# Gated attention, GLU and routed experts in one kernel: three kinds of work moved from POOL to VectorE, and the routing pieces placed anew in the order of the groups

## The chip, the cores and the metric

The kernel runs on one core of a Trainium2 chip. Its time is the device time of one execution in microseconds (us); the time before is the median of three executions. Engines are named as in the profile: PE is TensorE (its weight loads are PEld), DVE is VectorE, ACT is ScalarE, POOL is GpSimd, SP is SyncE.

## The reference

Three layers follow one another on 3072 tokens (4 batches of 768) of width 384 (8 heads of 48), all in float32.

```python
for t in range(S):                                        # gated linear attention
    state = alpha[:, :, t, :, None] * state + np.einsum('bhd,bhe->bhde', k[:, :, t], v[:, :, t])
    y[:, :, t] = np.einsum('bhd,bhde->bhe', q[:, :, t], state)
...
x = ((x @ w_a) * (x @ w_b)) @ w_out                       # GLU, 384 -> 1536 -> 384
...
logits = x @ w_gate + modality_bias[modality_id]          # 8 experts, the best one takes the token
out[mask] = gate_w[mask, None] * (np.maximum(x[mask] @ w1[e], 0.0) @ w2[e])   # 384 -> 1024 -> 384
```

## The kernel before

Float32 products are made of three TensorE passes: each operand is split into a high part (a copy in fp32r on ACT, names ending in h) and a remainder (a subtraction, names ending in l), and high times high, high times low and low times high are summed.

**Groups.** The tokens are cut into eight groups (w = 0 to 7) of 384, each of three chunks of 128. A group goes through attention chunk by chunk and then through the GLU in 12 f-steps. An f-step has 18 matmuls `ab` (L723: x times 128 columns of w_a and of w_b), a copy `asb` of the first half (ACT, L728), the product `g` (DVE, L734), its high part `gh` (ACT, L736) and remainder `gl` (DVE, L741), and nine matmuls `px` of w_out (L693), which come one f-step later. Group 7 has no attention left beside it; after it come the experts.

**Order.** PE, DVE, ACT and SP execute in the order in which the code issues, and that order is written by hand in strings: SEQ for groups 0 to 2, STEADY once for each of groups 2 to 6. A line of STEADY is an f-step of group w; four lines hold a chunk of group w+1's attention, and the pieces of group w-1's routing are strewn in. The letters: m is `ab`, `asb`; p is `px`; g is `g`, `gh`; l is `gl`. The numbers 1, 2, 3 prepare a chunk on DVE: transposes of alpha, k and q (L397), the running products R (L419) and `at` (L430), `kt` (L428) and `qt` = q times `at` (L432). S is the scores `s` = `kt` by `qt` on PE (L444). M masks them to `sm`. V is the part on the state: in before the pads (`vpad`, ACT, L471), the decay `state` times R (L477) and `y` (PE, L492 to L513). H is `xh`, the high part of `y` (ACT, L525) and the transposed keys on PE (L535); X is its remainder `xl` (DVE, L529); T is `ktok` (ACT, L537); U is `u` (PE, L543) and its addition to the state (DVE, L559); D closes the chunk.

**Routing, R.** Each R is one piece of `route` (L764). For groups 1 to 5 (and 6, in a form of its own below) a logit is a product with a row of the gate matrix, summed along the row on DVE (`junk`, L771; 24 for a group, two to a piece). Then come the softmax and the one-hot choice `oh` (DVE, L789 to L810, one piece), the counts `rank` on PE (L815 to L819, one piece), and the positions `rk`, `posi`, `base` on DVE (L823 to L829) with three indirect DMAs by POOL (L832) that write the tokens' places into a table in HBM. Groups 0 and 7 make the logits on PE: three transposes `xT`, a copy on ACT, three small matmuls `L` for each 128 tokens (L779 to L786).

**Group 7 and the experts.** The table of groups 0 to 6 is read back (`rte`, SP, L1019) when group 6 has been routed. The first expert weights `w1re`, `w2re` are issued on SP behind that read; ACT makes their high parts (`w0he` to `w3he`, L1067), between the `asb` and `gh` of group 7; the remainders (L1068) are made on DVE, every fourth one on POOL. Three early slots of experts and nine late ones follow.

Of the kernel before, what the change touches and what calls it, by code (L numbers as in the profile page):

```python
# [20 lines left out]
P = 128  # L21
# [45 lines left out]
MIX = 5, 2, 3  # L67
# [6 lines left out]
def gla_moe_kernel(ctx, tc, q, k, v, alpha, w_a, w_b, w_out, modality_id, w_gate, modality_bias, w1, w2, out):  # L74
# [162 lines left out]
    def load_ids():  # L237
# [5 lines left out]
        idf = ap.tile([NT, P], F32, tag="sm", bufs=3, name="idf")  # L243
# [11 lines left out]
        t0 = ap.tile([P, NT, E], F32, tag="sm", bufs=3, name="bias0")  # L255
# [67 lines left out]
    class Attention:  # L323
# [79 lines left out]
        def prepare(self, c):  # L403
# [28 lines left out]
            (nc.vector if self.w < LATE else nc.gpsimd).tensor_tensor(qt, q0, at, op=ALU.mult)  # L432
# [40 lines left out]
        def decay(self, c):  # L473

            if self.gc(c):
                R = self.ready[c][0]
                (nc.gpsimd if self.w else nc.vector).tensor_tensor(  # L477
                    state, state, R.broadcast_to([P, NPAIR, 2 * D]), op=ALU.mult
                )

        def values(self, c):
# [7 lines left out]
            if later:  # L489
                for kk in range(2):  # L490
                    for i in range(2):
# [3 lines left out]
                        if not (kk or i or self.w < LATE):  # L495
# [165 lines left out]
    def tokens(*groups):  # L661
# [15 lines left out]
        names = dict(S=["scores"], M=["mask"], V=["pads", "decay", "values"], H=["high"], X=["low"], T=["keys"], U=["carry"], D=["add"])  # L677
        return {**{nm.upper(): turns(nm) for nm in "akq"}, **dict.fromkeys("123", p), **{t: each(*does) for t, does in names.items()}}

    def lazily(make):  # L680
        yield from make()
# [82 lines left out]
    def route(w, pool, puts, gate=None):  # L764
# [3 lines left out]
        for t in range(CPW):  # L768
# [7 lines left out]
            else:  # L776
# [3 lines left out]
                xt = pool.tile([P, 512], F32, tag="sm", bufs=3, name=f"xT{w}_{t}")[:, :DM]  # L780
# [227 lines left out]
    class Slot:  # L1008
# [44 lines left out]
        def split(self):  # L1053
# [3 lines left out]
            for j in range(2 * NF2):  # L1057
# [10 lines left out]
                (nc.gpsimd if j % 4 == 3 else nc.vector).tensor_tensor(l, src, h, op=ALU.subtract)  # L1068
# [171 lines left out]
    def clear_table():  # L1240
        fill = ap.tile([P, TAB // P * 2], F32, tag="sm", bufs=3, name="fill")
# [3 lines left out]
    def turn_gate():  # L1245
# [4 lines left out]
        t = ap.tile([P, 512], F32, tag="sm", bufs=3, name="gateT")[:E, :DM]  # L1250
# [3 lines left out]
    def pipeline(y_d=None):  # L1254
# [3 lines left out]
        with tc.tile_pool(name="att", bufs=1) as ap:  # L1258
# [19 lines left out]
            if y_d is None:  # L1278
                with tc.manual_schedule(engines={EN.DVE, EN.PE, EN.SP, EN.Activation}):
# [7 lines left out]
                    def second():  # L1287
# [5 lines left out]
                        clear_table()  # L1293
# [28 lines left out]
                    extra = {"r": rest, "i": load_ids(), "W": gate_turn(), "Z": chain(then_load(then), then_load(nxt)), "R": lazily(lambda: route(0, ap, puts))}  # L1322
                    todo = halves + [(w, f) for w in range(2, NW - 1) for f in range(NF)]
# [30 lines left out]
                    for w in range(2, NW - 1):  # L1354
# [200 lines left out]
```

## Time and profile before

| what | value |
|---|---|
| median of three executions | 867.98 us (867.7 to 869.49) |
| the profiled execution | 876.44 us |
| its span in the trace | 874.6 us, so 1.8 us lie outside the span |
| PE, DVE, ACT, POOL busy | 819.8, 674.0, 292.7, 206.0 us |
| chain of work that ended last | PE 61%, DVE 21%, issue 6%, ACT 3%, POOL 3%, DMA 2% |

The busy times are sums over the whole span; whether an engine waits in a stretch, and for whom, is read from the views of the waits and from the timeline. Durations are those of the one profiled execution, which took 8.5 us longer than the median.

### The profile page before, as it was taken

Reading aid. Unit: us, or ns where it says so; the run is one execution under the profiler, and the core shown is the slowest. Engines: PE = TensorE matmul, PEld = TensorE weight load, DVE = VectorE, ACT = ScalarE, POOL = GpSimd, SP = SyncE. Lnnn points to the kernel's source line nnn. Section 1 sums busy time; section 2 is a strip of 40 time slices with the busy share of each in tenths; the row PEclk is TensorE's granted clock in tenths of the full one; section 3 lists DMA queues with packets and bytes.
Section 4 is the critical chain, followed back from the end, with each engine's and each line's share of the span. In section 5 each row is a group of like instructions: output and inputs, shape, how many; then the busy total and the mean of one; then the engine's idle time right before and its main releaser. Section 6 shows DMA issues by size and latency. Waiting matters only on the chain.

```text
span 874.6 us, 16828 instructions
## 1 busy us (share of the span) xinstructions
PE 819.8 (94%) x6193; PEld 771.2 (88%) x6193; DVE 674.0 (77%) x1495; ACT 292.7 (33%) x684; POOL 206.0 (24%) x283
## 2 busy tenths in 40 slices
PE   7778999999999998999999999899799999999995
PEld 6667998988998998998899899899699998998994
DVE  7878898659887987998998888774569876675641
ACT  2233442331222222221222222121555565564640
POOL 5221100102111012111111111102426554555421
PEclk9899999999999999999999999999899999999998
DMA  9988842716412410422422220030943988695900
GB/s 170 195 191 201 209 123 73 195 52 81 110 28 63 107 50 2 136 56 54 118 64 64 62 59 1 2 100 2 385 130 137 326 313 275 184 362 162 314 33 23
DMA packets 127089, 113.93 MB, mean 130 GB/s; under 512 B 55919, under 2 KB 105875, under 8 KB 126996
## 3 DMA queue, kind: packets, MB, share of 16 engines
q1 hardware_dynamic: 116260, 100.57, 42.2%
q0 software_dynamic: 4480, 10.99, 3.6%
q10 hardware_dynamic: 6256, 1.19, 1.1%
q8 instruction: 51, 0.84, 0.5%
q14 instruction: 42, 0.34, 0.1%
HBM read 101.87 MB, written 11.00 MB: 129 GB/s over the span
## 4 chain that ended last, share of the span: by engine, by line
PE 61%; DVE 21%; issue 6%; ACT 3%; POOL 3%; DMA 2%; another core or an unknown queue 2%; SPq 1%; DVEq 0%; POOLq 0%; ACTq 0%
PE ab L723 19%; PE px L693 9%; PE hl L1155 9%; PE pol L1103 8%; DVE R L419 3%; DVE at L430 2%; DVE g L734 2%; PE he L1155 2%; PE poe L1103 2%; PE s L444 2%; PE u L543 2%; DVE junk L771 2%; DVE kt L397 2%; DVE qt L397 1%
## 5 line engine op out<-in xcount | busy, mean ns | idle before, releaser
L723 PE MATMUL ab<-xh,pa 128*128 128x384 f32 x576 | 166.0, 342 | 7.9 <-ACT asb L728 5.5
L723 PE MATMUL ab<-xh,pb 128*128 128x384 f32 x576 | 163.4, 337 | 3.5 <-DVE pb L225 2.8
L693 PE MATMUL px<-po,gh 128*128 128x384 f32 x576 | 148.3, 342 | 0.4 <-DVE po L225 0.4
L723 PEld LDWEIGHTS ab<-xh,pa 128*128 128x128 f32 x576 | 106.4, 189 | 9.6 <-ACT asb L728 5.8
L723 PEld LDWEIGHTS ab<-xh,pb 128*128 128x128 f32 x576 | 106.1, 189 | 5.4 <-DVE pb L225 3.7
L736 ACT ACTIVATE gh<-g 128x384 fp32r<-128x384 f32 x96 | 50.3, 524 | 172.7 <-DVE g L734 171.4
L693 PEld LDWEIGHTS px<-po,gh 128*128 128x128 f32 x576 | 101.8, 188 | 3.8 <-issue 1.0
L723 PE MATMUL ab<-xl,pa 128*128 128x384 f32 x288 | 97.2, 337 | 0.3
L723 PE MATMUL ab<-xl,pb 128*128 128x384 f32 x288 | 96.8, 336 | 0.0
L728 ACT ACTIVATE asb<-ab 128x384 f32<-128x384 f32 x96 | 46.9, 489 | 145.5 <-PE ab L723 143.5
L693 PE MATMUL px<-po,gl 128*128 128x384 f32 x288 | 94.4, 337 | 0.3 <-DVE gl L741 0.3
L734 DVE TENSOR_TENSOR g<-ab,asb 128x384 f32<-128x384 f32 x96 | 53.2, 554 | 50.6 <-issue 26.7
L1160 DVE SCALAR_TENSOR_TENSOR hll<-hl,hhl 128x256 fp32r<-128x256 f32 x72 | 30.3, 421 | 54.1 <-ACT hhl L1158 50.4
L771 DVE SCALAR_TENSOR_TENSOR junk<-xr,gate 128x384 bf16<-128x384 f32 x96 | 65.2, 679 | 2.4
L477 POOL TENSOR_TENSOR state<-state,R 128x384 f32<-128x384 f32 x18 | 16.1, 895 | 203.1 <-DVE R L419 193.9
L741 DVE TENSOR_TENSOR gl<-g,gh 128x384 fp32r<-128x384 f32 x96 | 54.0, 563 | 9.7 <-ACT gh L736 9.7
L723 PEld LDWEIGHTS ab<-xl,pa 128*128 128x128 f32 x288 | 54.6, 190 | 0.8 <-DVE xl L529 0.8
L693 PEld LDWEIGHTS px<-po,gl 128*128 128x128 f32 x288 | 53.8, 188 | 1.0 <-DVE gl L741 1.0
L723 PEld LDWEIGHTS ab<-xl,pb 128*128 128x128 f32 x288 | 54.5, 189 | 0.0
L1158 ACT ACTIVATE hhl<-hl 128x256 fp32r<-128x256 f32 x72 | 27.7, 384 | 63.4 <-PE hl L1155 55.0
L832 POOL DMA_INDIRECT tab_d<-rec,posi x24 | 24.2, 1009 | 89.7 <-DVE base L829 50.1
L432 POOL TENSOR_TENSOR qt<-qt,at 128x512 f32<-128x512 f32 x15 | 20.3, 1355 | 89.3 <-DVE qt L397 89.3
(340 smaller groups left out, 1871.4 us busy)
## 6 DMA issues: line engine op xcount, KB each, us to landing
w1rl<-in_moe_w SPq DMA_DIRECT2D x18, 768.0 KB
w2rl<-in_moe_w SPq DMA_DIRECT2D x18, 768.0 KB
raw_a<-in_alpha SPq DMA_DIRECT2D x72, 96.0 KB
raw_k<-in_k SPq DMA_DIRECT2D x72, 96.0 KB
raw_q<-in_q SPq DMA_DIRECT2D x72, 96.0 KB
wo<-in_moe_w_out SPq DMA_DIRECT2D x6, 768.0 KB
w1re<-in_moe_w SPq DMA_DIRECT2D x6, 768.0 KB
w2re<-in_moe_w SPq DMA_DIRECT2D x6, 768.0 KB
```

The source lines that it names most:

```text
L397: nc.vector.transpose(t.rearrange("p a (r n) -> p a n r", n=self.TPP), self.raws.pop((nm, c)).rearrange("p a (n d) -> p a n d", d=D)[:, :, ...
L693: newest["mm"] = nc.tensor.matmul(px[w][t][:, :DM], a_, b_, start=(first and i == 0), stop=(last and i == 2))
L723: nc.tensor.matmul(pt[:, :WIN], a_, b_, start=(i == 0), stop=(i == 3 * KD - 1))
L728: nc.scalar.activation(asb, pt[:, :WIN], AF.Copy)
L734: nc.vector.tensor_tensor(g, pab[1][:, :WIN], asb, op=ALU.mult)
L736: newest["act"] = nc.scalar.activation(gh, g, AF.Copy)
L741: newest["gl"] = nc.vector.tensor_tensor(gl, g, gh, op=ALU.subtract)
L771: nc.vector.scalar_tensor_tensor(junk, xr[w][t], 1.0, gate[e], op0=ALU.mult, op1=ALU.mult, accum_out=L[:, t, e : e + 1])
L1103: newest["mm"] = nc.tensor.matmul(self.po[t][:, :DM], a_, b_, start=(f == 0 and i == 0), stop=(f == NF2 - 1 and i == 2))
L1155: nc.tensor.matmul(pt[:, :n], a_, b_, start=(i == 0), stop=(i == 3 * KD - 1))
L1158: nc.scalar.activation(gh[:, :n], pt[:, :n], AF.Relu)
L1160: nc.vector.scalar_tensor_tensor(gl[:, :n], pt[:, :n], 0.0, gh[:, :n], op0=ALU.max, op1=ALU.subtract)
```

## The change

- `qt` (L432) is multiplied on DVE in every group; before, DVE did it for groups 0 to 2 and POOL for groups 3 to 7.
- The decay of the state (L477) is on DVE in every group; before, on POOL from group 1 on. With the pads it has a letter of its own, E, ahead of M; V is `y` alone.
- The mask of group 2 is made on DVE as in the later groups; before, by a copy on ACT and a selection on POOL.
- All remainders of expert weights (L1068) are made on DVE.
- T stands ahead of V and H, so the keys go through PE ahead of `y`.
- Routing pieces are strewn otherwise: in lines 5 and 9 of STEADY stands one more piece; the softmax piece comes in line 10 ahead of m's products, `rank` as the one piece of line 11, and `rk` with the indirect DMAs after D of line 12.
- Clearing the table (a fill and a DMA on POOL) comes at a letter C in the GLU of group 1 and no longer in the start.
- FINAL: the first four f-steps of group 7 are issued in the hand order too, and group 6's routing, four to six f-steps earlier in group 7, makes its logits on PE (nine transposes, nine small matmuls, three ACT copies) in place of 24 `junk` instructions on DVE; `rank` of group 6 comes in f-step 4 instead of 6, and ACT meets `w0he` after `gh` of f-step 7 instead of 8.

```diff
 STEADY = (
     "m p g 1 l 2"
     "m p g 3 l R R"
-    "m S p g R l M R R"
-    "m V H T p U g 1 X l D"
-    "m p g 1 l 2"
+    "m S p g R l E M R R"
+    "m T V H p U g 1 X l D"
+    "m p g 1 l 2 R"
     "m p g 3 l R R"
...
-    "m p g 1 l 2"
-    "m p g 3 l R R Z Z"
-    "m S p g R l M R R"
-    "m V H T p U g 0 X l D Y"
+    "m p g 1 l 2 R"
+    "m p g 3 l R Z Z"
+    "m S p g l E M R"
+    "m T V H p U g X l 0 D R Y"
+)
+FINAL = (
+    "m p g l"
+    "m p R g l R"
+    "m R p g R l R"
+    "m p R g l R"
 )
...
-MIX = 5, 2, 3
+MIX = 1, 2, 2
...
-            (nc.vector if self.w < LATE else nc.gpsimd).tensor_tensor(qt, q0, at, op=ALU.mult)
+            nc.vector.tensor_tensor(qt, q0, at, op=ALU.mult)
...
-                if self.w < LATE:
+                if self.early:
                     nc.scalar.activation(sm, pv, AF.Copy)
...
-                (nc.gpsimd if self.w else nc.vector).tensor_tensor(
-                    state, state, R.broadcast_to([P, NPAIR, 2 * D]), op=ALU.mult
-                )
+                nc.vector.tensor_tensor(state, state, R.broadcast_to([P, NPAIR, 2 * D]), op=ALU.mult)
...
-        names = dict(S=["scores"], M=["mask"], V=["pads", "decay", "values"], H=["high"], X=["low"], T=["keys"], U=["carry"], D=["add"])
+        names = dict(S=["scores"], M=["mask"], E=["decay", "pads"], V=["values"], H=["high"], X=["low"], T=["keys"], U=["carry"], D=["add"])
...
-                (nc.gpsimd if j % 4 == 3 else nc.vector).tensor_tensor(l, src, h, op=ALU.subtract)
+                nc.vector.tensor_tensor(l, src, h, op=ALU.subtract)
...
-                        clear_table()
...
+                    late_route = route(NW - 2, ap, puts)
+                    emit(FINAL, {"R": late_route})
```

**Order of DVE, chunk 1 of group 3.** Here group 3's second chunk is prepared beside f-steps 4 and 5 of group 2; `junk` x2 is one routing piece. First the rows of before.

```order
L741 TENSOR_TENSOR gl2_4_2651<-g2_4_2639,gh2_4_2641 128x384
L397 STREAM_TRANSPOSE kt3_1_2653<-raw_k3_1_2220 128x4x4x32
L428 TENSOR_TENSOR kt3_1_2653<-kt3_1_2653,R3_1_2645 128x512
L734 TENSOR_TENSOR g2_5_2687<-ab2_5_1_2668,asb2_5_2666 128x384
L430 SCALAR_TENSOR_TENSOR at3_1_2597<-at3_1_2597,starts_146 128x516
L397 STREAM_TRANSPOSE qt3_1_2692<-raw_q3_1_2225 128x4x4x32
L741 TENSOR_TENSOR gl2_5_2695<-g2_5_2687,gh2_5_2689 128x384
L771 SCALAR_TENSOR_TENSOR junk_85,L1_2457<-xs1_1_2233,gate1_1774 128x384 x2
```

The same place after the change.

```order
L750 TENSOR_TENSOR gl2_4_2645<-g2_4_2633,gh2_4_2635 128x384
L403 STREAM_TRANSPOSE kt3_1_2647<-raw_k3_1_2209 128x4x4x32
L434 TENSOR_TENSOR kt3_1_2647<-kt3_1_2647,R3_1_2639 128x512
L778 SCALAR_TENSOR_TENSOR junk_85,L1_2451<-xs1_1_2222,gate1_2330 128x384 x2
L743 TENSOR_TENSOR g2_5_2683<-ab2_5_1_2664,asb2_5_2662 128x384
L436 SCALAR_TENSOR_TENSOR at3_1_2591<-at3_1_2591,starts_146 128x516
L403 STREAM_TRANSPOSE qt3_1_2688<-raw_q3_1_2214 128x4x4x32
L438 TENSOR_TENSOR qt3_1_2688<-qt3_1_2688,at3_1_2591 128x512
L750 TENSOR_TENSOR gl2_5_2691<-g2_5_2683,gh2_5_2685 128x384
```

A routing piece has come in ahead of `g2_5`, and `qt3_1`'s product stands behind its transpose. In chunk 2 (f-steps 8 and 9) it is the same; in chunk 0 only the product is added.

**Order of DVE, f-step 10 of group 2.** `oh1` is group 1's choice, which `rank1` on PE reads; `rank1` stands on PE at the same place in both orders, after `px` of f-step 9. First the rows of before.

```order
L806 TENSOR_TENSOR oh1_3028<-mr1_3026,rank8_91 128x24
L808 TENSOR_REDUCE se1_3030<-ex1_3021 128x3
L809 TENSOR_SCALAR se1_3030<-se1_3030 128x3
L810 RECIPROCAL rec_105<-se1_3030 128x3
L741 TENSOR_TENSOR gl2_10_3034<-g2_10_3013,gh2_10_3015 128x384
L464 TENSOR_TENSOR sm3_2_0_3036<-s3_2_0_2994,cmask_82 128x512
L464 TENSOR_TENSOR sm3_2_1_3038<-s3_2_1_2995,cmask_82 128x512
L823 TENSOR_TENSOR rk1_3047<-rank1_3040,base_95 128x24
L824 TENSOR_TENSOR rk1_3047<-rk1_3047,oh1_3028 128x24
L826 TENSOR_REDUCE pos1_3050<-rk1_3047 128x3
L828 CAST posi1_3052<-pos1_3050 128x3
L829 TENSOR_TENSOR base_95<-base_95,rank1_3040 128x8
```

The same place after the change.

```order
L813 TENSOR_TENSOR oh1_2943<-mr1_2941,rank8_91 128x24
L815 TENSOR_REDUCE se1_2945<-ex1_2936 128x3
L816 TENSOR_SCALAR se1_2945<-se1_2945 128x3
L817 RECIPROCAL rec_105<-se1_2945 128x3
L743 TENSOR_TENSOR g2_10_3024<-ab2_10_1_2995,asb2_10_2993 128x384
L750 TENSOR_TENSOR gl2_10_3028<-g2_10_3024,gh2_10_3026 128x384
L483 TENSOR_TENSOR state_133<-state_133,R3_2_2878 128x384
L470 TENSOR_TENSOR sm3_2_0_3033<-s3_2_0_3005,cmask_82 128x512
L470 TENSOR_TENSOR sm3_2_1_3035<-s3_2_1_3006,cmask_82 128x512
L743 TENSOR_TENSOR g2_11_3101<-ab2_11_1_3056,asb2_11_3054 128x384
L533 TENSOR_TENSOR xl3_2571<-y3_2_3066,xh3_2570 128x3x128
L750 TENSOR_TENSOR gl2_11_3106<-g2_11_3101,gh2_11_3103 128x384
```

The softmax piece now stands ahead of `g2_10` (it stood behind it), the decay is in the row, and `rk1` to `base` (and with `posi1` POOL's indirect DMAs) have gone behind `gl2_11` and the first transpose of the next chunk.

**Order of ACT in group 7, at the first expert weight.** `w0he0` needs the first expert weight from HBM. First the rows of before.

```order
L728 ACTIVATE asb7_7_6802<-ab7_7_0_6792 128x384
L736 ACTIVATE gh7_7_6825<-g7_7_6823 128x384
L728 ACTIVATE asb7_8_6851<-ab7_8_0_6841 128x384
L736 ACTIVATE gh7_8_6874<-g7_8_6872 128x384
L1067 ACTIVATE w0he0_6878<-w1re0_0_6722 128x384 x4
L728 ACTIVATE asb7_9_6898<-ab7_9_0_6888 128x384
L736 ACTIVATE gh7_9_6921<-g7_9_6919 128x384
```

The same place after the change.

```order
L737 ACTIVATE asb7_7_6813<-ab7_7_0_6803 128x384
L745 ACTIVATE gh7_7_6836<-g7_7_6834 128x384
L1074 ACTIVATE w0he0_6840<-w1re0_0_6684 128x384 x4
L737 ACTIVATE asb7_8_6860<-ab7_8_0_6850 128x384
L745 ACTIVATE gh7_8_6883<-g7_8_6881 128x384
L1074 ACTIVATE w1he0_6887<-w1re0_1_6686 128x384 x4
L737 ACTIVATE asb7_9_6907<-ab7_9_0_6897 128x384
```

`w0he0` has moved one f-step forward, and `asb7_8` instead of `asb7_9` stands behind it. `rank6` has moved two f-steps forward (from the `ab` of f-step 6 to that of f-step 4).

## Rows read from the trace of the kernel before

**Rows 1.** The page: busy us, share of the span, instructions.

```profile
PE 819.8 (94%) x6193; PEld 771.2 (88%) x6193; DVE 674.0 (77%) x1495; ACT 292.7 (33%) x684; POOL 206.0 (24%) x283
```

**Rows 2.** Waits of PE, 75 to 660 us: total, times, longest.

```profile
PE rank L815 <- DVE oh L806: 6.6, 6, 1.1
PE ab L723 <- ACT asb L728: 5.5, 1, 5.5
PE s L444 <- POOL qt L432: 4.9, 13, 1.1
PE ab L723 <- ACT xh L525: 2.5, 3, 0.8
PE u L543 <- ACT ktok L537: 1.8, 2, 0.9
```

**Rows 3.** Timeline of DVE, group 1's softmax piece: first and last instruction.

```profile
262.79 0.17 DVE L789 TENSOR_TENSOR L<-L,bias_all 128x24 f32<-128x24 f32 x1
...
264.58 0.18 DVE L810 RECIPROCAL rec<-se 128x3 f32<-128x3 f32 x1
```

**Rows 4.** Timeline of ACT: `xh` of two chunks of group 3.

```profile
220.72 0.49 ACT L525 ACTIVATE xh<-y 128x384 fp32r<-128x384 f32 x1 [2.57 <-PE y L513]
...
271.71 0.49 ACT L525 ACTIVATE xh<-y 128x384 fp32r<-128x384 f32 x1 [4.52 <-remote]
```

**Rows 5.** Timeline of PE around the second of these.

```profile
269.07 0.62 PE L513 MATMUL y<-sm,vpad 128*32 128x128 f32 x16
...
272.25 0.45 PE L723 MATMUL ab<-xh,pa 128*128 128x384 f32 x1 [0.80 <-ACT xh L525]
272.84 0.44 PE L723 MATMUL ab<-xl,pa 128*128 128x384 f32 x1
```

**Rows 6.** Timeline of POOL: first and last of group 1's indirect DMAs.

```profile
267.40 1.02 POOL L832 DMA_INDIRECT tab_d<-rec,posi  x1 [7.06 <-DVE base L829]
...
270.00 0.97 POOL L832 DMA_INDIRECT tab_d<-rec,posi  x1 [0.30 <-issue]
```

**Rows 7.** Groups by line and form: duration ns min/median/max, first and last start.

```profile
L432 POOL TENSOR_TENSOR qt<-qt,at x15: 1343/1357/1359, 211.4 to 550.7; 128x512 f32<-128x512 f32 x15
L432 DVE TENSOR_TENSOR qt<-qt,at x3: 691/692/694, 148.9 to 183.9; 128x512 f32<-128x512 f32 x3
L477 POOL TENSOR_TENSOR state<-state,R x18: 832/837/1579, 38.2 to 545.0; 128x384 f32<-128x384 f32 x18
L477 DVE TENSOR_TENSOR state<-state,R x2: 559/682/805, 21.8 to 26.5; 128x384 f32<-128x384 f32 x2
L424 DVE TENSOR_TENSOR starts<-starts,once x18: 166/754/785, 141.7 to 545.1; 128x4 f32<-128x4 f32 x18
L771 DVE SCALAR_TENSOR_TENSOR junk<-xs,gate x24: 546/557/1541, 211.6 to 261.8; 128x384 bf16<-128x384 f32 x24
```

**Rows 8.** Windows, busy us by engine, PEclk, DMA share, GB/s: chunk 1 of group 3.

```profile
226.94:250.68 23.74, 23.45 (x186) 22.39 (x185) 21.24 (x49) 5.34 (x12) 2.30 (x3) 1.00 0.23 59
```

**Rows 9.** The same view, 18 `ab` matmuls of group 7 behind the longest wait.

```profile
617.53:623.38 5.85, 5.85 (x18) 5.85 (x19) 4.21 (x5) 2.67 (x6) 3.11 (x3) 0.51 1.05 391
```

**Rows 10.** Timeline of ACT: the first copy of an expert weight.

```profile
615.34 1.76 ACT L1067 ACTIVATE w0he<-w1re 128x384 fp32r<-128x384 f32 x4 [8.30 <-DMA w1re<-in_moe_w]
```

**Rows 11.** Timeline of PE: routing of group 0 through PE.

```profile
165.13 0.49 PE L779 MATMUL xT<-ident,xs 128*128 128x128 f32 x3
166.26 0.83 PE L785 MATMUL L<-wg_sb,xT 128*128 128x8 f32 x6 [0.64 <-ACT xT L781]
```

**Rows 12.** The start: POOL's timeline, waits of PE 24 to 75 us, window 25 to 50 us.

```profile
28.18 0.77 POOL L1243 DMA_DIRECT2D tab_d<-fill  x1 [5.97 <-issue]
...
PE y L508 <- POOL sm L462: 3.6, 4, 1.8
...
25.00:50.00 25.00, 19.46 (x182) 16.56 (x175) 19.60 (x35) 5.84 (x11) 5.37 (x8) 0.86 0.88 184
```

**Rows 13.** Waits of PE in the expert stage, 660 to 865 us.

```profile
PE poe L1103 <- DVE hle L1160: 1.4, 3, 0.7
```

More of the change, by code (lines that the diff above doesn't have):

```diff
@@ L242, in load_ids @@
         yield
-        idf = ap.tile([NT, P], F32, tag="sm", bufs=3, name="idf")
+        idf = ap.tile([P, UNIT // 2], F32, tag="cv", bufs=4, name="idf")[:NT, :P]
         nc.vector.tensor_copy(idf, idr.rearrange("t (p w) -> t p w", w=2)[:, :, 0])
@@ L494, in values @@
                         )
-                        if not (kk or i or self.w < LATE):
+                        if not (kk or i or self.early):
                             for n in ("mask", "pads"):
@@ L676, in tokens, with features @@
         p = chain.from_iterable(a.prepare(c) for a in groups for c in range(CPW))
-        names = dict(S=["scores"], M=["mask"], V=["pads", "decay", "values"], H=["high"], X=["low"], T=["keys"], U=["carry"], D=["add"])
+        names = dict(S=["scores"], M=["mask"], E=["decay", "pads"], V=["values"], H=["high"], X=["low"], T=["keys"], U=["carry"], D=["add"])
         return {**{nm.upper(): turns(nm) for nm in "akq"}, **dict.fromkeys("123", p), **{t: each(*does) for t, does in names.items()}}
+    def features(pieces):
+        for piece in pieces:
+            if piece in "le":
+                yield
     def lazily(make):
-        yield from make()
+        yield from make() or ()
     def products(work_list):
@@ L748, in moe @@
     def moe(w):
-        for piece in products([(w, f) for f in range(NF)]):
-            if piece in "le":
-                yield
+        return features(products([(w, f) for f in range(NF)]))
     def gate_columns(name, pool, n, **tag):
@@ L1240, in clear_table @@
     def clear_table():
-        fill = ap.tile([P, TAB // P * 2], F32, tag="sm", bufs=3, name="fill")
+        fill = ap.tile([P, UNIT // 2], F32, tag="cv", bufs=4, name="fill")[:, : TAB // P * 2]
         nc.gpsimd.memset(fill, BIG)
@@ L1299, in gate_turn @@
                         turn_gate()
+                        yield
                         gate.append(gate_columns("gate", ap, 2, tag="cv", bufs=4))
@@ L1320, in late_steps @@
                         yield
-                    extra = {"r": rest, "i": load_ids(), "W": gate_turn(), "Z": chain(then_load(then), then_load(nxt)), "R": lazily(lambda: route(0, ap, puts))}
-                    todo = halves + [(w, f) for w in range(2, NW - 1) for f in range(NF)]
+                    extra = {"r": rest, "i": load_ids(), "C": lazily(clear_table), "W": gate_turn(), "Z": chain(then_load(then), then_load(nxt)), "R": lazily(lambda: route(0, ap, puts))}
+                    todo = halves + [(w, f) for w in range(2, NW) for f in range(NF)]
                     joint = products(todo)
@@ L1358, in pipeline @@
                         emit(STEADY, {**groups[w + 1], **kinds, "0": groups[w + 2]["1"]})
-                        assert not any(True for _ in chain(*(groups[w + 1][c] for c in "1SMVHXTUD"), *kinds.values()))
+                        assert not any(True for _ in chain(*(groups[w + 1][c] for c in "1SMEVHXTUD"), *kinds.values()))
                     assert next(rest, None) is None
-                    assert next(joint) == "e"
+                    late_route = route(NW - 2, ap, puts)
+                    emit(FINAL, {"R": late_route})
             else:
@@ L1375, in pipeline @@
             nc.vector.tensor_reduce(fold, ident.rearrange("p (j c) -> p c j", c=TINY), axis=AX.X, op=ALU.add)
-            last = moe(NW - 1)
-            gate = gate_columns("last", m2, 4, tag="wr", bufs=6) if y_d is None else None
-            run((islice(last, 1), 1))
             early = []
-            run((islice(last, MIX[0]), 1), (behind(chain(route(NW - 2, m2, puts, gate), early_table(early))), 2))
+            if y_d is None:
+                last, routing, n = features(joint), late_route, MIX[0]
+            else:
+                last, routing, n = moe(NW - 1), route(NW - 2, m2, puts), NF // 2
+            run((islice(last, n), 1), (behind(chain(routing, early_table(early))), 2))
             slots = [Slot(f"e{i}", "e", i, 2, (NW - 1) * WIN) for i in range(NEARLY)]
```

6 lines of the change are left out of this document (3 added, 3 removed), and 26 rows, old and new, of tables (SEQ, STEADY).

## The prediction

> **What bounds the kernel now.** I read first how busy the engines are: PE works 94% of the span [rows 1], so little can be won but where PE waits, and the next question is for whom. The view of PE's waits answers it: between 75 and 660 us five entries hold 21.3 us [rows 2]. Then the timelines, to see what lies before each of these waits, and a window on one chunk of the attention, to see whether DVE, which gets the work, has room: in 23.74 us PE is busy 23.45 and DVE 21.24 [rows 8]. DVE is therefore close behind PE, and an instruction added there is free only as long as 2.2 us per chunk last.
>
> **The rank wait.** PE waits six times for `oh`, 6.6 us in all [rows 2]: `rank` has its place in PE's order behind `px` of f-step 9, and DVE makes the ten softmax instructions only then, for example from 262.79 to 264.76 us, two us in a row [rows 3]. After, the piece stands ahead of `g` of f-step 10, behind an f-step that has lost its two routing pieces, while `rank` stays; DVE is done with `oh` before PE has come through the scores and `px`. Five of the six are in the groups so ordered; group 0's stays. Gain 5/6 of 6.6 = 5.5 us. If the piece made `g` late instead, the gain would be 0 (a rival).
>
> **The late end of `y`.** ACT's `xh` reads `y`. In the first chunk of group 3 the wait ends with PE's `y`; in the last the last matmul of `y` ends at 269.69 us and `xh` starts at 271.71, 2.0 us later, and the releaser named is "remote" [rows 4, 5]. The same 2.0 us stand in the last chunk of groups 3 to 7, and in no other of the chunks behind group 2. What those five have and the others lack: POOL issues three indirect DMAs between 267.40 and 270.97, exactly over `y` [rows 6]. I take it that PE's signal is held up until they have gone, without knowing why. PE pays 2.5 us in front of `ab` and 1.8 in front of `u` [rows 2], and after a wait for `xh` the second matmul also starts late: 0.59 us after the first [rows 5], where a step takes 5.85 x 0.51 / 18 = 0.17 us at full clock [rows 9]; three times 0.42 is 1.3. After, `rk` to `posi` stand behind D, so the DMAs fall into the `ab` of the next group's first f-step, where PE's signals go to buffers with time in hand. Gain 2.5 + 1.8 + 1.3 = 5.6 us; 0 if they hold up the next signal just as dearly.
>
> **`qt` and the decay on DVE.** PE's scores wait for POOL's `qt` 13 times, 4.9 us, 1.1 at most; the other twelve have 0.32 on average [rows 2]. POOL needs 1.36 us for what DVE does in 0.69 [rows 7], so `qt` comes about 0.7 us sooner behind its transpose, which would clear them. But in chunks 1 and 2 a routing piece has come in ahead: two `junk` of 0.56, 1.2 us with what lies between. And DVE gets time back: L424, 0.17 us by its fastest row, takes 0.75 where POOL's decay runs, and the `junk` beside POOL's `qt` takes 1.54 for 0.56 [rows 7]. Ahead of `qt` in chunk 1 that makes -0.67 (faster) + 1.2 - 0.58 = -0.05: as late as before. In chunk 0, without the piece, it is 1.25 sooner. So I count chunk 0 alone, the 1.1 and four of 0.32: 2.4 us. Bounds: 0, and 4.9.
>
> DVE's account for chunk 1: 21.24 [rows 8] + 0.69 + 0.56 (decay) + 1.2 (its sixth piece) - 0.98 - 0.58 = 22.1 us, against 23.45 of PE. Covered, with 1.3 us left; should the decay take the 0.81 of its slower row [rows 7], 1.1 are left. The mask of group 2 and the earlier T and E have the same cover, and I cost them at nothing.
>
> The Trainium skill ("SBUF — State Buffer", Who interferes with whom) says that a DVE instruction with two SBUF inputs and a GpSimd instruction that reads SBUF exclude each other for the whole instruction. The stretched rows of L424 and `junk` agree with it; its result for the sum is the fourth rival.
>
> **The turn to the experts.** ACT stands at `w0he` for 8.30 us until the first weight is there [rows 10], `asb` is queued behind it, and PE waits 5.5 us for `asb` [rows 2]: ACT may wait 8.3 - 5.5 = 2.8 us before PE feels it. Behind the gap the granted clock is 0.51, the lower of its two levels (1.2 of 2.4 GHz), and 18 `ab` take 5.85 us [rows 9] instead of 5.85 x 0.51 = 3.0: another 2.9. After, `rank6` stands about two and a half f-steps earlier; an f-step is 27 matmuls of 0.17 us, 4.7 us, so 11.7. The routing through PE, all ahead of it, costs 0.49 for `xT` and 0.42 (half of 0.83, six matmuls) for `L` in each of three tiles, and a wait of 0.64 for the first copy, as group 0 shows [rows 11]: 2.7 + 0.64 = 3.4 us. Net, table and weights come 11.7 - 3.4 = 8.3 us earlier; ACT is at `w0he` 4.7 - 3.4 = 1.3 earlier. Its wait falls from 8.3 to 8.3 - (8.3 - 1.3) = 1.3 us, under the 2.8. PE no longer stands and the clock should hold: 5.5 + 2.9 - 3.4 = 5.0 us gained. If the weights are more than 1.5 us later than that, part of both losses returns; with none of it gained the term is -3.4.
>
> **Start and experts.** In the start PE waits 3.6 us for masks by POOL, which sits 5.97 us in the table's clearing DMA [rows 12]; that DMA and the decays leave the stretch. But DMA is busy to 0.88 there [rows 12], so what PE gains may be lost waiting for the weights of the next f-step. Between 0 and 3.6 I take 2. In the expert stage PE waits 1.4 us for DVE's remainders of h [rows 13]; a weight remainder on DVE is a 128x384 subtraction, 0.56 us by the decay's fastest row of that shape [rows 7]. Eight more per expert are 4.5 us of DVE, less what it no longer loses beside POOL; between 0 and 1.4, half: 0.7.
>
> **Sum.** 5.5 + 5.6 + 2.4 + 5.0 + 2 + 0.7 = 21.2 us from the profiled 876.4: 855.2. The median was 868.0, 1% below the profiled execution; 21.2 x 0.99 = 21.0, so 847.0 us.
>
> **Rivals.** (1) DVE becomes the bound, and it ends slower. Place: chunk 1 of each group first, f-steps 4 to 7. If nothing comes back from the ended contention, and `qt` takes POOL's 1.36 and the decay 0.81, a chunk has 21.24 + 1.36 + 0.81 + 1.2 = 24.6 us of DVE against 23.45, 1.2 over; as the 2.5 us in which DVE now stands (23.74 - 21.24) are waits for PE's products, which stay in part, I add half, 1.25: 2.4 us x 15 chunks = 36, 847 + 36 = 883. It decides from 21 / 15 = 1.4 us per chunk on. For it: only 1.3 us of margin. Against it: DVE's own `qt` rows say 0.69, and the stretched rows are plain. The Trainium skill ("Perfetto Trace Analysis", Optimizing Scalar/DVE Operations) speaks against moving work onto a saturated DVE: it would rather offload it, to GpSimd too, though it adds that the shared port may undo the benefit. This case's trace has DVE busy for 0.89 of the chunk [rows 8], so near it but not there.
>
> (2) The weights come late all the same: ACT at `w0he` is one f-step earlier, and its margin is 1.5 us. The 8.4 us are not gained: 847 + 8.3 = 855.
>
> (3) The change does not do what it says at `rank` or `y`: the softmax piece delays `g` and so `gl`, and PE waits the same 5.5 at `px`; or the late signal goes with the indirect DMAs to another place (5.6). Either gives 852 to 853, both 858.
>
> (4) More than forecast: if POOL's 0.84 and 1.36 were lost to DVE whole [rows 7], 2.2 us come back per chunk instead of 1.56, `qt` is 0.6 sooner in chunks 1 and 2 too, and all 4.9 us go: 2.5 more than counted, 844.5. For it: the stretched rows end with POOL's. Against it: what they lost is 0.58 and 0.98. The rule of the Trainium skill named above is this case's ground.
>
> **How the numbers follow.** Forecast 0.55 (its own range 843 to 851, from start and experts at their bounds and `qt` from 0 to 2.4); rival 4 0.08; rival 2 0.13; rival 3 0.13; rival 1 0.11, of which 0.07 reach the slower side and 0.04 end near no change. A measurement of this kernel can tell about 0.2%, 1.7 us, from no change. Faster 0.89, same 0.04, slower 0.07. The range goes from 840 (rival 4 with start and experts at their bounds) to 857 (rival 2 with 2 us less elsewhere).
>
> **What would show it.** Right: no POOL rows of `qt`, state and L1068; PE's wait for `oh` once instead of six times; `xh` starting within 0.1 us of `y` in the last chunks; no wait of several us for `asb` around f-step 9 of group 7 and a granted clock of 1.00 between 600 and 640; waits for `qt` left, at 0.3, in chunks 1 and 2. Wrong: PE waiting for `g`, `gl` or DVE's `qt` in every chunk, DVE at over 0.95 of a chunk, or ACT's `w0he` row again with several us in front.

## The result, and the profile after

The changed kernel takes 847.83 us (median of four, 847.05 to 849.65), the kernel before 868.74 on the same chip: ratio 0.976, with an interval of 0.974 to 0.979. It is faster, and the forecast was 847.0.

The page after, first part, answers to [rows 1]: PE is busy 96% of a shorter span, POOL has lost 91 us, DVE has not gained any.

```profile
PE 814.3 (96%) x6220; PEld 773.4 (91%) x6220; DVE 661.0 (78%) x1537; ACT 291.4 (34%) x681; POOL 114.9 (14%) x196
```

The waits of PE after, 75 to 640 us (total, times, longest), answer to [rows 2]. The entries for `asb`, `xh`, `ktok` and POOL's `qt` are gone; `rank` waits once, and `qt`, now DVE's, six times. The waits for `xT` and `gl` have grown from one each (0.6 and 0.3 us before) to two.

```profile
PE s L450 <- DVE qt L438: 2.0, 6, 0.5
PE rank L822 <- DVE oh L813: 1.5, 1, 1.5
PE L L792 <- ACT xT L788: 1.2, 2, 0.6
PE px L702 <- DVE gl L750: 0.8, 2, 0.4
```

Where the waits for `qt` lie is read from PE's timeline. Before, those of chunks 0 and 1 of group 3:

```profile
212.77 1.16 PE L444 MATMUL s<-qt,kt 64*128 64x128 f32 x16 [1.14 <-POOL qt L432]
...
236.50 1.16 PE L444 MATMUL s<-qt,kt 64*128 64x128 f32 x16 [0.29 <-POOL qt L432]
```

After, chunk 0 of group 3 and chunk 1 of group 4. The other waits of chunk 0 (groups 6 and 7) are 0.51 and 0.54 us, those of chunk 1 (groups 5 and 6) 0.15 and 0.16, and chunk 2 has none.

```profile
206.12 1.16 PE L450 MATMUL s<-qt,kt 64*128 64x128 f32 x16 [0.54 <-DVE qt L438]
...
298.43 1.16 PE L450 MATMUL s<-qt,kt 64*128 64x128 f32 x16 [0.15 <-DVE qt L438]
```

The last chunk of group 3 after, from the timelines of PE, ACT and POOL: `y` ends at 261.46 and `xh` starts 0.06 us later, released by `y`, where it was 2.0 us [rows 4, 5]; the indirect DMAs come behind it, beside `ab`. First PE's row, then ACT's, then POOL's.

```profile
260.84 0.62 PE L517 MATMUL y<-sm,vpad 128*32 128x128 f32 x16
```

```profile
261.52 0.49 ACT L529 ACTIVATE xh<-y 128x384 fp32r<-128x384 f32 x1 [2.86 <-PE y L517]
```

```profile
266.40 1.06 POOL L839 DMA_INDIRECT tab_d<-rec,posi  x1 [13.00 <-DVE base L836]
```

The groups by line and form (duration in ns, min/median/max) answer to [rows 7]: with nothing of POOL beside them, L430 (L424 before) and `junk` have no stretched row left. The window is chunk 1 of group 3 [rows 8]: DVE is busy 21.9 of 23.6 us and PE 23.46.

```profile
L438 DVE TENSOR_TENSOR qt<-qt,at x18: 691/693/694, 142.7 to 534.6; 128x512 f32<-128x512 f32 x18
L483 DVE TENSOR_TENSOR state<-state,R x20: 547/553/683, 21.7 to 539.2; 128x384 f32<-128x384 f32 x20
L430 DVE TENSOR_TENSOR starts<-starts,once x18: 166/167/169, 135.5 to 528.5; 128x4 f32<-128x4 f32 x18
L778 DVE SCALAR_TENSOR_TENSOR junk<-xs,gate x24: 547/557/561, 206.4 to 249.3; 128x384 bf16<-128x384 f32 x24
```

```profile
225.70:249.30 23.60, 23.46 (x186) 22.48 (x185) 21.89 (x55) 5.46 (x12) 0.10 (x1) 1.00 0.23 58
```

At the turn ACT comes to `w0he` and the weight is there (no idle in front of the row, 8.30 us in [rows 10]); PE is busy without a break and the granted clock is full, 0.51 in [rows 9].

```profile
586.55 1.75 ACT L1074 ACTIVATE w0he<-w1re 128x384 fp32r<-128x384 f32 x4
```

```profile
583.00:608.00 25.00, 25.00 (x153) 24.93 (x152) 14.07 (x29) 12.92 (x30) 6.65 (x10) 1.00 0.97 363
```

In the expert stage PE no longer waits for DVE [rows 13], but for tokens gathered by DMA (waits after, 640 to 840 us).

```profile
PE xtl L656 <- DMA xgl<-x_d,gil: 2.6, 2, 1.8
```

Where the time came from is seen best by when PE starts the same matmul in both traces (start of a row of PE's timeline, us):

| PE starts | before | after | gained so far |
|---|---|---|---|
| first `ab` of all | 36.77 | 30.92 | 5.9 |
| group 2, f-step 0 | 198.30 | 192.63 | 5.7 |
| group 7, f-step 0 | 564.14 | 545.16 | 19.0 |
| group 7, f-step 4 | 583.40 | 567.68 | 15.7 |
| group 7, f-step 8 | 602.46 | 586.83 | 15.6 |
| first `hl` (first late expert slot) | 690.78 | 662.56 | 28.2 |
| end of the span | 874.6 | 847.9 | 26.7 |

The profiled executions differ by 26.8 us (876.44 and 849.65), the medians by 20.9, because the profiled one of before lay 7.7 us above the median of 868.74 and that of after 1.8 above its own. The table tells of the profiled pair.

### The profile page after: what moved, and what is told of

Its sections match the earlier page's. It is cut to its first block, busy times and chain, and to the rows that moved or that the text cites. A ratio compares the mean times of both kernels' runs of the same rounds, so it can differ in the third digit from the quotient of the medians.

```text
span 847.9 us, 16735 instructions
## 1 busy us (share of the span) xinstructions
PE 814.3 (96%) x6220; PEld 773.4 (91%) x6220; DVE 661.0 (78%) x1537; ACT 291.4 (34%) x681; POOL 114.9 (14%) x196
## 4 chain that ended last, share of the span: by engine, by line
PE 77%; DVE 9%; DMA 5%; issue 4%; SPq 2%; POOL 1%; ACT 1%; POOLq 0%; DVEq 0%; ACTq 0%
PE ab L732 29%; PE px L702 15%; PE hl L1162 8%; PE pol L1110 7%; PE he L1162 3%; PE poe L1110 3%; PE s L450 3%; DMA wb<-in_moe_w_b 2%; PE u L547 2%; PE y L496 1%; DMA xgl<-x_d,gil 1%; PE y L512 1%; PE y L517 1%; DVE R L425 1%; SPq L370 1%
## 5 line engine op out<-in xcount | busy, mean ns | idle before, releaser
L702 PE MATMUL px<-po,gh 128*128 128x384 f32 x576 | 150.6, 343 | 0.0
L702 PE MATMUL px<-po,gl 128*128 128x384 f32 x288 | 96.4, 338 | 0.8 <-DVE gl L750 0.8
L778 DVE SCALAR_TENSOR_TENSOR junk<-xr,gate 128x384 bf16<-128x384 f32 x96 | 53.3, 556 | 2.2
L417 POOL MEMSET at<- 128x4 f32 x24 | 2.5, 105 | 325.7 <-DVE qt L438 325.7
L450 PEld LDWEIGHTS s<-qt,kt 64*128 64x128 f32 x384 | 24.7, 193 | 10.4 <-PE ab L732 7.2
```

Of the source, the lines that this page charges most:

```text
L450: nc.tensor.matmul(pts[g][:, i * P : (i + 1) * P], kt[o : o + 64, i, :], qt[o : o + 64, i, :], start=True, stop=True)
L702: newest["mm"] = nc.tensor.matmul(px[w][t][:, :DM], a_, b_, start=(first and i == 0), stop=(last and i == 2))
L778: nc.vector.scalar_tensor_tensor(junk, xr[w][t], 1.0, gate[e], op0=ALU.mult, op1=ALU.mult, accum_out=L[:, t, e : e + 1])
```

## The experiments

All times are medians, with the ratio to the kernel before on the same chip; that kernel's median was 873.3, 874.4 and 866.9 us on three chips (that of E1 to E4; of the control, E6, E7 and E10; of E5, E8, E11 and E12), while the changed kernel gave 847.8 in the first result and 847.5 as the control. So the experiments on the changed kernel are compared with 847.5 to 847.8, and where one or two us matter, by their traces.

| run | time, us | ratio | interval |
|---|---|---|---|
| control: the changed kernel again | 847.52 | 0.969 | 0.968 to 0.970 |
| E1 clearing in the start | 848.14 | 0.971 | 0.970 to 0.973 |
| E2 DMAs beside `y` | 859.06 | 0.984 | 0.983 to 0.985 |
| E3 softmax piece late | 847.42 | 0.971 | 0.970 to 0.972 |
| E4 `qt`, decay on POOL | 866.15 | 0.992 | 0.991 to 0.994 |
| E5 every fourth remainder on POOL | 848.93 | 0.980 | 0.977 to 0.982 |
| E6 routing one step later | 854.75 | 0.977 | 0.976 to 0.979 |
| E7 routing on VectorE | 851.07 | 0.973 | 0.972 to 0.974 |
| E8 fewer waits | 843.07 | 0.973 | 0.971 to 0.975 |
| E10 before, with `qt`, decay on VectorE | 890.78 | 1.016 | 1.014 to 1.019 |
| E11 old spread of logits | 849.35 | 0.980 | 0.978 to 0.982 |
| E12 E10, decay ahead of mask | 855.29 | 0.988 | 0.985 to 0.990 |

**Control.** 

> The changed kernel as it is, for a time on the same chip as the three runs beside it. Both theories: 847 to 849 us, and a ratio to the kernel before between 0.970 and 0.979, as wide as its first result and the neighbours of the first call.

The time came as expected, the ratio at 0.969 just under the band, as the kernel before was slower on that chip.

**E2: do the indirect DMAs hold up `y`?**

```diff
-    "m S p g l E M R"
-    "m T V H p U g X l 0 D R Y"
+    "m S p g l E M R R"
+    "m T V H p U g X l 0 D Y"
```

> The changed kernel with the last routing piece of each group (positions and the three indirect DMAs) one place earlier, at the end of line 11 of STEADY, so that POOL's DMAs lie beside the y of the last chunk again; nothing else moves. Theory: y's end is held up by about 2 us, xh starts 2 us late in the last chunks of groups 3 to 7, and PE loses about 1.1 us in each: 5 to 6 us in all, about 853. Rival: the late end had another cause (the ranks, the order of keys); then xh follows y within 0.1 us and the time stays at 847.8.

11 us over E1 and E3 on the same chip, twice the 5 to 6 expected. POOL, ACT and PE in the last chunk of group 3, each from its timeline: the DMAs lie over `y` again, `y` ends at 260.46, `xh` starts 2.6 us later with "remote" as its releaser, and PE waits 1.42 us for it. After that wait the clock falls too: the last 16 of the f-step's 18 `ab` matmuls have a granted clock of 0.61 and take 4.33 us, where 16 steps of 0.17 us at full clock are 2.7. Before's wait of 0.80 left the clock at 1.00.

```profile
258.81 0.97 POOL L839 DMA_INDIRECT tab_d<-rec,posi  x1 [6.42 <-DVE base L836]
...
261.36 0.97 POOL L839 DMA_INDIRECT tab_d<-rec,posi  x1 [0.30 <-issue]
```

```profile
263.10 0.49 ACT L529 ACTIVATE xh<-y 128x384 fp32r<-128x384 f32 x1 [5.43 <-remote]
```

```profile
263.64 0.44 PE L732 MATMUL ab<-xh,pa 128*128 128x384 f32 x1 [1.42 <-ACT xh L529]
```

```profile
264.51:268.84 4.33, 4.33 (x18) 4.33 (x17) 2.44 (x4) 0.49 (x1) 0.00 (x0) 0.61 0.01 4
```

The order of PE is the same as in the changed kernel, and group 2's f-steps before this point take the same time to 0.04 us. By the starts of the f-steps E2 loses 3.7 us in each of groups 3, 5 and 7, which have this wait and the fall of the clock, and 0.8 in groups 4 and 6, which have neither. In all fifteen late chunks of before, E2 and E10, `xh` starts 0.74 to 0.84 us after the row of the last of the three DMAs ends, however long `y` has been done. That the DMAs beside `y` make its end late in these runs is shown; how they do it is not, and E12 below has them beside `y` without it.

**E3 and E11: what made PE wait at `rank`?** E3 puts the softmax piece back behind `g`; E11 also gives the logit pieces their old lines.

```diff
 E3
-    "m p g 3 l R Z Z"
-    "m S p g l E M R"
+    "m p g 3 l Z Z"
+    "m S p g R l E M R"
 E11, against the changed kernel
-    "m p g 1 l 2 R"
+    "m p g 1 l 2"
...
-    "m p g 1 l 2 R"
-    "m p g 3 l R Z Z"
-    "m S p g l E M R"
+    "m p g 1 l 2"
+    "m p g 3 l R R Z Z"
+    "m S p g R l E M R"
```

> The changed kernel with the softmax piece back in line 11, directly ahead of the scores' px, and the rank still in line 11. Theory: PE waits 1.1 us for the one-hot choice in each of five groups, 5.5 us, about 853, and the DMAs stay harmless. Rival: the wait was hidden by what stands behind it (g and gl come sooner without the piece ahead of them); then less than 2 us are lost.

> The changed kernel with the logit pieces of chunks 1 and 2 and the softmax piece where they stood before (two logit pieces in line 10, softmax behind g in line 11), rank and the indirect DMAs as changed. Theory: what made PE wait for the choice was the load of VectorE ahead of it, two logit pieces of 1.2 us each with what contention added, not the place behind g; with them back PE waits about 1 us in each of five groups: 4 to 6 us above the control, 852 to 853. Rival: with qt and the decay no longer on POOL the load is small enough in any order: within 1.5 us of the control.

E3 changes nothing, as its rival said. DVE ends `oh` at 252.85 us, and PE comes to `rank` at 253.23 (timelines).

```profile
252.67 0.18 DVE L813 TENSOR_TENSOR oh<-mr,rank 128x24 bf16<-128x24 f32 x1
```

```profile
253.23 0.19 PE L822 MATMUL rank<-oh,tri_b 128*128 128x24 bf16 x1
```

In E11 the waits are back (its waits of PE), six of them, 0.7 in each of the five groups beside group 0's 1.5. They cost 0.65 us a group in f-step 10; 0.2 come back in chunk 1, where `qt` no longer stands behind a logit piece: 0.45 us a group, 2.1 in the five, and 1.8 over the control by the medians of different chips, under half of the 4 to 6 expected. So the load ahead of the choice makes the wait, not the piece's place behind `g`. Of the 1.1 us of before, 0.7 hang on the spread; the other 0.4 go when `qt` and the decay leave POOL, for E10 and E12 below have the old order and 0.7 a group too.

```profile
PE rank L822 <- DVE oh L813: 5.0, 6, 1.5
```

**E4, E10 and E12: `qt` and the decay.** E4 puts both back on POOL in the changed kernel. E10 is the kernel before with both on VectorE and nothing else. E12 is E10 with one more line.

```diff
 E4
-            nc.vector.tensor_tensor(qt, q0, at, op=ALU.mult)
+            (nc.vector if self.w < LATE else nc.gpsimd).tensor_tensor(qt, q0, at, op=ALU.mult)
...
-                nc.vector.tensor_tensor(state, state, R.broadcast_to([P, NPAIR, 2 * D]), op=ALU.mult)
+                (nc.gpsimd if self.w else nc.vector).tensor_tensor(state, state, R.broadcast_to([P, NPAIR, 2 * D]), op=ALU.mult)
 E12, against E10
-        names = dict(S=["scores"], M=["mask"], V=["pads", "decay", "values"], H=["high"], X=["low"], T=["keys"], U=["carry"], D=["add"])
+        names = dict(S=["scores"], M=["decay", "mask"], V=["pads", "values"], H=["high"], X=["low"], T=["keys"], U=["carry"], D=["add"])
```

> The changed kernel with qt (groups 3 to 7) and the decay (groups 1 to 7) back on POOL, the order unchanged. Theory: PE waits for qt in every chunk; with the extra routing piece ahead in chunks 1 and 2 it comes about 1.2 us later than before there, so the loss is more than the 2.4 us counted: 15 chunks, 4.9 us of waits as before plus up to 1 us in ten chunks, 4 to 14 us, about 855. Rival: DVE was the bound of those chunks and is relieved; then the time stays at 847.8 or falls.

> The kernel before with one part of the change alone: qt and the decay on VectorE, every order as it was. Theory: qt comes 0.7 us sooner and VectorE gets back 1.6 us per chunk, so the 4.9 us of waits for qt go and the waits for the one-hot choice shrink: 4 to 8 us under the kernel before. Rival: VectorE is full and the two instructions delay g and the choice as much; then no change or slower than the kernel before.

> The kernel before with qt and the decay on VectorE, as in the run that was slower than before, but with the decay ahead of the mask instead of behind it and the two routing pieces. Theory: the late decay alone made that run slow (PE waits 18.7 us for it, and at the lower clock after some of the waits), so it goes: 890.8 falls by 20 us or more, to 5 to 8 us under the kernel before, about 867. Rival: VectorE is full and the wait moves on to the mask, the choice or g: 875 to 890.

E4 loses 18.4 us against E1 and E3 on the same chip, more than the whole band of 4 to 14 that was expected. Its waits of PE and its groups by line: 17.9 us for POOL's `qt`, three to four times that of before, and L430 and `junk` are stretched as in [rows 7].

```profile
PE s L450 <- POOL qt L438: 17.9, 14, 1.4
```

```profile
L430 DVE TENSOR_TENSOR starts<-starts,once x18: 166/750/780, 134.8 to 543.2; 128x4 f32<-128x4 f32 x18
L778 DVE SCALAR_TENSOR_TENSOR junk<-xs,gate x24: 547/558/1531, 205.4 to 251.6; 128x384 bf16<-128x384 f32 x24
```

E10, the same part alone in the old order, is 16.3 us slower than before by the medians (two of its six executions took 885.5 and 885.8 us): its rival, on the slower side. Its waits of PE name the place. Then rows of DVE's and PE's timelines and a window: the decay stands behind the mask and the last logit pieces of line 11 (`junk` at 222.61 to 224.88, decay at 224.88), and PE's `y` waits 2.74 us for it; behind such waits the clock falls here too (0.82 in the 9.4 us from 225.58).

```profile
PE y L492 <- DVE state L477: 18.7, 10, 2.7
PE rank L815 <- DVE oh L806: 4.5, 6, 0.9
```

```profile
224.88 0.55 DVE L477 TENSOR_TENSOR state<-state,R 128x384 f32<-128x384 f32 x1
```

```profile
225.58 0.78 PE L492 MATMUL y<-qt,state 128*64 128x128 f32 x8 [2.74 <-DVE state L477]
```

```profile
225.58:235.00 9.42, 9.42 (x87) 8.59 (x88) 4.58 (x10) 2.00 (x4) 0.00 (x0) 0.82 0.27 67
```

E12 moves the decay ahead of the mask and falls from 1.016 to 0.988 of before: 25 us by the ratios, 35.5 by medians of two chips. It is 11.6 us under before on its chip, more than the 5 to 8 expected. No wait of `y` for the state is left behind 75 us. It still waits at `rank` and for `asb`.

```profile
PE rank L815 <- DVE oh L806: 4.5, 6, 0.9
PE ab L723 <- ACT asb L728: 3.6, 1, 3.6
```

One thing more is gone in E12 that was not touched: the waits for `xh` and `ktok`, 2.8 and 2.0 us in E10. POOL's indirect DMAs lie beside `y` as before, but `xh` follows `y` by 0.06 or 0.07 us in all five chunks. In the last chunk of group 3 (timelines of PE, POOL and ACT):

```profile
262.70 0.62 PE L513 MATMUL y<-sm,vpad 128*32 128x128 f32 x16
```

```profile
261.50 0.97 POOL L832 DMA_INDIRECT tab_d<-rec,posi  x1 [7.99 <-DVE base L829]
262.78 0.98 POOL L832 DMA_INDIRECT tab_d<-rec,posi  x1 [0.30 <-issue]
```

```profile
263.39 0.49 ACT L525 ACTIVATE xh<-y 128x384 fp32r<-128x384 f32 x1 [2.57 <-PE y L513]
```

E12 ran on another chip than E2 and E10 and has another order than both, so the runs do not tell which of the two ends the delay. What the decay's place is worth is therefore better read from the ratios than from the medians.

**E6 and E7: the turn to the experts.** E6 takes group 6's routing later in group 7. E7 makes its logits on VectorE again, with the gate rows that the earlier groups used.

```diff
 E6
-    "m p R g l R"
-    "m R p g R l R"
-    "m p R g l R"
+    "m p g l"
+    "m p R g l R"
+    "m R p g R l R"
 E7
-    "m p g l"
-    "m p R g l R"
-    "m R p g R l R"
-    "m p R g l R"
+    "m p g l R R"
+    "m p R g R l R"
+    "m p R g R l R"
+    "m p R g R l R"
...
-                    late_route = route(NW - 2, ap, puts)
+                    late_route = route(NW - 2, ap, puts, gate[0])
```

> The changed kernel with group 6's routing put about one and a half f-steps later in group 7 (rank at the end of f-step 5 instead of in f-step 4). Theory: the first expert weights land about 7 us later while ACT comes to its first copy at the same time, so ACT waits about 7 us, PE about 7 - 2.8 = 4 us for asb, and 2 to 3 us more at the lower clock: 852 to 855. Rival: the gain at the turn comes from the place of the expert copy in ACT's order and not from the routing's time; then the time stays within 2 us of the control.

> The changed kernel with group 6's logits made on VectorE again (24 products summed along the row, with the gate rows of the earlier groups), as early in group 7 as VectorE allows, instead of through TensorE. Theory: PE is spared 3.3 us of transposes, but VectorE needs 14 us for the products, the rank comes about one f-step later relative to the group's start, and the wait for the weights takes back as much: 847 to 852. Rival: the detour through TensorE is a pure cost; then 844.5, 3.3 us under the control.

E6 costs 7.2 us. ACT (timeline) waits 8.12 us at `w0he` and PE (waits, 540 to 620 us) 5.3 for `asb`: the slack between the two is 2.8 us, as worked out from before. E7 costs 3.5: PE is spared the transposes, but `w0he` waits 9.08 us and PE 6.3. Rows of E6 (timeline, waits):

```profile
592.59 1.76 ACT L1074 ACTIVATE w0he<-w1re 128x384 fp32r<-128x384 f32 x4 [8.12 <-DMA w1re<-in_moe_w]
```

```profile
PE ab L732 <- ACT asb L737: 5.3, 1, 5.3
```

The same two of E7:

```profile
590.36 1.76 ACT L1074 ACTIVATE w0he<-w1re 128x384 fp32r<-128x384 f32 x4 [9.08 <-DMA w1re<-in_moe_w]
```

```profile
PE ab L732 <- ACT w0he L1074: 6.3, 1, 6.3
```

**E1: the clearing of the table.**

```diff
                         load_weights(1, "ab")
+                        clear_table()
...
-                    extra = {"r": rest, "i": load_ids(), "C": lazily(clear_table), "W": gate_turn(), "Z": chain(then_load(then), then_load(nxt)), "R": lazily(lambda: route(0, ap, puts))}
+                    extra = {"r": rest, "i": load_ids(), "C": iter(()), "W": gate_turn(), "Z": chain(then_load(then), then_load(nxt)), "R": lazily(lambda: route(0, ap, puts))}
```

> The changed kernel with the clearing of the table put back into the start. Theory: POOL sits about 6 us in that DMA while group 0's masks wait for it, and PE reaches the first f-step 5.9 us later, which nothing later absorbs: the time is 5 to 6 us above the changed kernel's 847.8 (about 853.5), in the profile PE waits about 2.4 us for POOL's masks again and the first ab starts near 36.8 instead of 30.9 us. Rival: the start gains come from the decay and the mask order, or are an effect of the profiled execution alone; then the timed result stays within 2 us of 847.8.

No loss. But the run does not undo what it was to undo: the fill has another buffer than in before, and POOL's order puts the DMA at 8.16 us, ahead of all masks (POOL's timeline), not between two of them as at 28.18 in [rows 12].

```profile
6.26 0.43 POOL L1249 MEMSET fill<- 128x388 f32 x1
8.16 0.78 POOL L1250 DMA_DIRECT2D tab_d<-fill  x1
```

It shows that the start needn't be free of the DMA. E10 and E12 keep the old start, with the DMA between masks: their first `ab` is at 35.4 and 35.1 us, where the changed kernel, the control and the nine runs made from it have 30.2 to 31.3.

**E5: the experts' remainders.**

```diff
-                nc.vector.tensor_tensor(l, src, h, op=ALU.subtract)
+                (nc.gpsimd if j % 4 == 3 else nc.vector).tensor_tensor(l, src, h, op=ALU.subtract)
```

> The changed kernel with every fourth expert remainder back on POOL. Theory: PE has almost no wait for VectorE in the expert stage (hl of slots apart by the same time before and after), so nothing is won or lost: within 1.5 us of the control's 847.5. Rival: the remainders beside POOL's hold VectorE up and PE waits again, 1 to 2 us above the control.

848.93 us: 1.1 to 1.4 us over the changed kernel's medians on other chips, which can't be told from nothing. The trace tells more: from the first `he` to the first `hl` PE takes 59.4 us and not 56.3, and waits for `hle`, the remainder of h, again (2.0 us, 1.4 at once). But its late slots then wait 0.2 us for gathered tokens and not 2.6. POOL's share costs 3 us in the early slots, and most of it is lost in the changed kernel to the next wait.

**E8: a faster order.**

```diff
 SEQ, groups 0 and 1 (five last lines)
-    "m p g 3 l R R"
-    "m S p g E M l 1 2 R"
-    "m T V H p U g X l 3 D R"
-    "m S p g E M l R R Z Z"
-    "m T V H p U g X 0 l D R W"
+    "m p g 3 l R"
+    "m R S p g E M l 1 2 R"
+    "m R T V H p U g X l 3 D R"
+    "m R S p g E M l Z Z"
+    "m T V H p U g X 0 l D R W"
 STEADY, last line
-    "m T V H p U g X l 0 D R Y"
+    "m T V H p U g 0 X l D R Y"
 FINAL
-    "m p R g l R"
-    "m R p g R l R"
-    "m p R g l R"
+    "m p R g l"
+    "m R p R g l"
+    "m R R p g l R R"
```

> The changed kernel with three waits that are left taken away by order alone: the routing of groups 0 and 6 is spread so that TensorE's matmuls stand between a transpose and its product, and between the choice and the rank (waits of 1.2 and 1.5 us), and the next group's first piece stands ahead of X again, so that the guards of the late loads do not delay g in groups 5 to 7 (1.5 us or so in two of them). Theory: 4 to 5 us under the control of 847.5, about 843. Rival: the routing of group 6 comes half an f-step later, the weights wait takes 2 us or more back, and xl comes late: 846 to 849.

843.07 us, 4.5 under the control's median and 5.9 under E5's on the same chip. By the starts of the f-steps against the first trace of the changed kernel, groups 5 and 6 give 1.35 and 1.15 us, and group 7's f-steps 0.8. Its waits of PE, 75 to 650 us, have no `xT` and no `gl`; ACT stands 1.74 us at `w0he`, under the slack.

```profile
PE s L450 <- DVE qt L438: 1.9, 8, 0.5
PE rank L822 <- DVE oh L813: 1.0, 1, 1.0
```

```profile
583.00 1.77 ACT L1074 ACTIVATE w0he<-w1re 128x384 fp32r<-128x384 f32 x4 [1.74 <-DMA w1re<-in_moe_w]
```

## Why the prediction was right, point by point

**The sum.** Rank, `y` and `qt` were to give 13.5 us; between f-step 0 of group 2 and of group 7 the traces give 19.0 - 5.7 = 13.3. Everything else gave 26.7 - 13.3 = 13.4 instead of 7.7. The forecast of the median is met to 0.8 us, but on the profiled pair it is 5.6 short (855.2 forecast, 849.65 measured). The two agree only because the profiled execution of before lay further above its median than that of after, so the closeness is luck. What made that execution 7.7 us longer is not settled; the kernel before has medians from 866.9 to 874.4 on different chips, the changed one does not follow them.

**The rank wait.** The gain is there, 5.1 us by the waits (6.6 to 1.5). The step "after, the piece stands ahead of `g`" gave the wrong reason: E3 undoes it at no cost. The other half of the sentence, the f-step that has lost its two routing pieces, carries it, with the contention that ended beside them (E11).

**The late end of `y`.** Right in place and size for the profiled pair: 4.3 us of waits are gone, and E2 brings them back and more. Rival 3's second half is out. But E12 shows that the late end does not come wherever the DMAs lie beside `y`. The kernel before took 866.9 us on E12's chip and 868.7 where the ratio was measured, against 873.3 and 874.4 on the chips of E2 and E10 and 876.4 in the profiled execution. It may therefore be that the 5.6 us lie in the profiled execution and not in the timed ones behind the ratio; no trace of a timed execution of the kernel before is there to show it.

**`qt` and the decay.** The waits fell by 2.9 us (4.9 to 2.0), near the 2.4 counted, but not where they were counted. Chunk 0, which was to be cleared, went only from 2.1 us (three waits) to 1.6 (three); chunks 1 and 2, which were to stay as late as before, went from ten waits of about 0.29, 2.8 us together, to three of 0.15 or 0.16. So the size is luck, and the sum for `qt` ahead of each chunk is wrong. In chunk 0 DVE has no idle row ahead of `qt` and stands behind work that only some groups have: 1.57 us of `xs` (L713) ahead of group 3, two reductions on `late` (L326, L327) of 0.74 us ahead of group 7. The sum left that out; no run takes it away to test it. Nor does the term say what the part is worth: with `qt` and the decay on POOL the new order is 18.4 us slower (E4), and with both on VectorE the old order is 16.3 slower (E10). The step that failed is "T and E have the same cover, and I cost them at nothing": E, the decay ahead of the mask, is worth 25 us or more once the decay is on VectorE (E10 to E12). I counted DVE's time in a chunk and not the time at which `y` needs the decay; 21.9 us of 23.6 are enough only in this order. Rival 1 was real, but at another place and with a smaller load than its price assumed.

Rival 4 is out in time, not in mechanism. The stretched rows end with POOL's work and return with it (E4). The Trainium skill ("SBUF — State Buffer", Who interferes with whom) states that a DVE instruction with two SBUF inputs contends with a GpSimd instruction that reads SBUF, and these runs agree: L430 takes 0.17 us without POOL's work and 0.75 with it. That all waits for `qt` would go did not follow.

**The turn.** Routing on PE cost 19.0 - 15.7 = 3.3 us (3.4 forecast), and the gap and its clock are gone. ACT waits 0 us where 1.3 were worked out, so rival 2 is out; the slack of 2.8 us that decided it is what E6 shows. By the first `hl` the turn had given 28.2 - 19.0 = 9.2 us and not 5.0: the further waits in the early slots (for `the`, the high part of the tokens, and for `hle`) went as well, 4.7 us from f-step 11 of group 7 to there, of which 0.7 was in the sum as the experts' term. Of that the late slots gave 1.5 back, waiting for gathered tokens. The eight further remainders per expert that the experts' term speaks of were four: POOL made 48 of 192 for twelve slots.

**The start.** 5.7 us against the 2 taken and a bound of 3.6. The term was mis-sized: the waits for masks counted, but not the low clock behind them (0.57 granted from 31 to 37 us before, 1.00 after) or what stands in line on PE, and the DMA share did not absorb the gain as I had supposed. That POOL's clearing between the masks is the cause is borne out by all runs with it and without it, but no run changed it alone. The start also differs between executions of one kernel: group 2 begins at 189.2 us in the control, 3.4 earlier than in the first trace.

## What to carry to other kernels

An instruction that changes engines needs its place changed with it: the same two multiplications cost 16 us in the old order and saved 12 when one of them moved ahead of the mask, each against the kernel before on the same chip. Count not only an engine's load in a period but when each consumer needs its result, and look at what is queued ahead of it. Where a wait is to be removed by reordering, undo the reorderings singly: two of the parts undone here (softmax ahead of `g`, remainders off POOL) moved the time by less than the medians tell.

## What the runs showed of the hardware

- Three indirect DMAs issued by POOL beside TensorE's `y` went with a late start of ACT on `y`: 2.0 to 2.7 us after the last matmul, and 0.74 to 0.84 us after the last DMA's row, in all fifteen such chunks of before, E2 and E10. In the five such chunks of E12, on another chip, it was 0.07 us, as it is at most in every chunk behind 75 us without such DMAs.
- A wait of PE of 1.42 us can cost as much behind it as in itself: the last 16 matmuls of that f-step took 4.33 us at a granted clock of 0.61, where full clock would be 2.7 (the turn of before has 18 in 5.85 us at 0.51, where full clock would be 3.0). Waits of 0.80 us at the same place left the clock at 1.00.
